# When sums and conversions are issued beside a chain of matrix products: one schedule change in a fused attention, mixture-of-experts and SoLU kernel

## Chip, cores and metric

The kernel runs on one core of one Trainium2 chip. The metric is device microseconds (us) of one execution, lower is better; several executions are timed and their median is given. TensorE is called PE in the profile, VectorE DVE, ScalarE ACT, GpSimd POOL, and SyncE, which only issues transfers here, SP.

## Reference, cut to what matters

Three layers follow one another: a local attention, a mixture of four experts in which every token goes through all experts, and a second layer with a softmax-gated normalisation. The change touches only how the weights of the last two layers are prepared.

```python
# mixture: N = 1536 tokens, D = 512, E = 4 experts, F = 1024
for e in range(E):
    h = np.maximum(x @ w1[e], 0.0)
    out += p[:, e:e + 1] * (h @ w2[e])
# second layer: its weights and g_ln arrive in float64
h = x @ w_in
...
return (ln @ w_out).astype(np.float32)      # ln = (solu - mu) / sqrt(var + 1e-06) * g_ln
```

## The kernel before

**Numbers in two parts.** Every product runs in three matmuls: each operand is split into a rounded high part and the rest (`split_of`, L275: the rounding is an ACT copy, L279, the rest a POOL subtraction, L287). A weight piece is 128 x 512; eight pieces make a half expert: four called R (first product, tiles `wR`) and four called V (second product, `wV`).

**A half expert.** `moe` (L598) walks over eight half experts, `he` = 0 to 7. For `he` of 1 and more the issue order is 23 groups of 12 matmuls, numbered 1 to 23 here. Groups 1 to 4 are the first product of the last 512 tokens (`g1`, L450); after each, ACT takes the rectified high part out of PSUM (L456) and VectorE the rest (L457). Groups 5 to 8 are the second product of the same tokens (`g2`, L469); it reads all four results, the fourth from its tenth and eleventh matmul on. VectorE scales what comes out of PSUM (L479) and POOL adds it to the running sum (L480). Groups 9 to 15 are the first product of the other 1024 tokens, done as seven products of half-size blocks instead of eight (`paired_groups`, L496, matmuls L530, evictions L517, L518, L535, L538). It needs sums and differences of weight blocks, the S pieces: `form_steps` (L312) loads two copies of weight pieces into `sc_b`, takes four sums on POOL (L328 to L331) and splits the two results (two ACT roundings, `ha` and `hb`, two POOL subtractions, `la` and `lb`). There are two such sets for each half expert. Groups 16 to 23 are the second product of those 1024 tokens, again L469, L479, L480.

**Conversions.** The second layer's weights arrive as 64-bit patterns. `conv_steps` (L341) brings 32 pieces to two-part form: load, four VectorE instructions (`one`, L189 to L192), three more (`two`, L196 to L198), for the last sixteen pieces a scaling by `gt` on ACT (L359), rounding on ACT (L360), the rest on VectorE (L363), store. Load and store are issued from ACT's queue.

**Order.** Each engine runs its instructions in the order in which the program issues them, so the order is written out by hand. After each group `tick` (L371) issues whatever side work is due: one step of each list in `st.work` (the S sets, and the splits of R and V pieces), loads of further pieces (`load_piece`, three raw buffers), loads of the second layer's weights (`load_second`) and, where the tick is not `quiet`, one step of each running conversion. Before the change the ticks of the paired groups are quiet except one, all others are not; a conversion starts every 3 or 4 ticks that are not quiet. Loads of weights, of S sets and of `pb` go through SP's queue. In the list of a half expert the first S set has its sums in tick 21 and its roundings in tick 22 and in tick 1 of the next half expert; the second set has its sums in tick 2 of the next half expert, its `ha` in tick 3 and its `hb` in tick 5.

Of the kernel before, what the change touches and what calls it, by code (L numbers as in the profile page):

```python
# [8 lines left out]
F32 = mybir.dt.float32  # L9
# [5 lines left out]
AF = mybir.ActivationFunctionType  # L15
# [35 lines left out]
def kernel(ctx, tc, ep, qk, vp, nn, pr, wall, w64, gl, out):  # L51
# [150 lines left out]
    def stream(arm):  # L202
# [9 lines left out]
        st.next_load = 0  # L212
        st.used = 0
        st.next_split = 0
        st.forms = []
        st.second = []
        st.free = {}
        st.hp = None
# [72 lines left out]
        def split_steps(hi_eng="act", lo_eng="pool", wait=0):  # L291

            if not ready(wait):
                return None
            n = st.next_split
            st.next_split += 1
            w = st.pieces[n] = place(n)
            steps = split_of(st.raws.pop(n), w, hi_eng, lo_eng)
            if n < 8:
                st.used += 1  # L300
                return steps

            def release():
                st.used += 1

            def both():
                for f in steps:
                    f()

            return [both, release]  # L310

        def form_steps(n):  # L312

            q = n % 8
            a, b = sc_b[q:q + 2]
            wa, wb = st.wS[:, q], st.wS[:, q + 1]
            st.pieces["S", n], st.pieces["S", n + 1] = wa, wb
            g, lo, hi = nc.gpsimd, slice(0, 256), slice(256, 512)

            def load():  # L320
                nc.sync.dma_start(out=a, in_=wall[n])
                nc.sync.dma_start(out=b, in_=wall[n + 1])

            def nothing():
                pass

            def sums():
                g.tensor_tensor(out=b[:, hi], in0=b[:, lo], in1=b[:, hi], op=ALU.add)  # L328
                g.tensor_tensor(out=b[:, lo], in0=a[:, lo], in1=b[:, lo], op=ALU.subtract)
                g.tensor_tensor(out=a[:, lo], in0=b[:, hi], in1=a[:, lo], op=ALU.subtract)  # L330
                g.tensor_tensor(out=a[:, hi], in0=a[:, hi], in1=a[:, lo], op=ALU.subtract)  # L331

            ha, la = split_of(a, wa, "act", "pool")
            hb, lb = split_of(b, wb, "act", "pool")
            return [load, nothing, nothing, sums, ha, la, hb, lb]

        def split_piece(hi_eng, lo_eng):
            for f in split_steps(hi_eng, lo_eng) or ():
# [2 lines left out]
        def conv_steps():  # L341

            c = st.next_conv
            if c >= 32 or st.cvp is None:
                return None
            st.next_conv += 1
            raw = st.cvp.tile([128, 256], I64, tag="r64", name=f"{arm}r64", bufs=2)
            one, two, ff, halves = from_f64(raw)

            def load():  # L350
                nc.scalar.dma_start(out=raw, in_=w64[c])

            def nothing():
                pass

            def high():
                if c >= 16:
                    j = (c - 16) // 2
                    nc.scalar.activation(ff, ff, AF.Copy, scale=gt[:, j:j + 1])  # L359
                nc.scalar.copy(halves[:, 0], ff)  # L360

            def low():
                nc.vector.tensor_tensor(out=halves[:, 1], in0=ff, in1=halves[:, 0].bitcast(F32), op=ALU.subtract)  # L363

            def store():
                nc.scalar.dma_start(out=w_dram[c // 2, :, :, 256 * (c % 2):256 * (c % 2) + 256], in_=halves.bitcast(F32))
                st.stored += 1

            return [load, nothing, one, two, high, low, store]

        def tick(split=True, quiet=False):  # L371

            st.now += 1
            for w in st.work:
                w.pop(0)()
            st.work = [w for w in st.work if w]
            if st.later and st.later[0][0] <= st.now:
                _, e, (c0, n) = st.later.pop(0)
                load_pb(e, c0, n)
            for at, n in st.forms:  # L380
                if at == st.now:
                    st.work.append(form_steps(n))
            if split:
                for _ in range(2):
                    w = split_steps(wait=2)
                    if w:
                        st.work.append(w)
            load_piece()
            load_piece()
            while st.second and st.stored >= 2 * st.second[0] + 2:  # L390
                load_second(st.second.pop(0))
            if not quiet:
                for w in st.conv:
                    w.pop(0)()
                st.conv = [w for w in st.conv if w]
                st.rest += 1
                if st.rest >= 4 - (st.next_conv % 2):
                    w = conv_steps()
                    if w:
                        st.conv.append(w)  # L400
                        st.rest = 0

        def drain():
            while st.work or st.second or st.conv:
                tick()

        st.tick = tick
# [88 lines left out]
        def paired_groups(he, h1, h2):  # L496
# [50 lines left out]
            for j in range(4):  # L547
                st.free["R", j] = he + 1
            if he < NHE - 1:
                st.forms += [(st.now + 2, 8 * he + 8), (st.now + 6, 8 * he + 10)]  # L550
            else:
                st.second += range(14)

# [32 lines left out]
                st.unformed.append(last)  # L586

        st.x_forms = x_forms
        st.paired_groups = paired_groups
        st.load_piece = load_piece  # L590
        st.split_piece = split_piece
# [6 lines left out]
    def moe(st, first_blocks):  # L598

        def run(he, blk, last, given=None):  # L600
            for gi, g in enumerate(st.gemm_groups(he, blk, last, given)):
                for cost in g:
                    yield 0, cost
                st.tick(st.wS is not None, quiet=he == 0)
            if he % 2 and he < NHE - 1:
                st.later.append((st.now + 2, he // 2 + 1, blk))

        for j, blk in enumerate(first_blocks):
            yield blk[0] + blk[1], 0.0
            if j == len(first_blocks) - 1:  # L610
                while st.unformed:
                    st.unformed.pop(0)()
            yield from run(0, blk, j == len(first_blocks) - 1)
        for he in range(1, NHE):
            yield from run(he, (2 * HALF, 512), False)
            h1, h2 = ([[None] * 4, [None] * 4] for _ in range(2))
            for i in st.paired_groups(he, h1, h2):
                yield 0, 0.0
                st.tick(quiet=i != 6)
            yield from run(he, (0, HALF), False, h1)  # L620
            yield from run(he, (HALF, HALF), True, h2)

    def rest_of_moe(st, arm, gen):
        with ExitStack() as es:
# [3 lines left out]
            st.ps3 = es.enter_context(tc.tile_pool(name=f"{arm}ps3a", bufs=1, space=PSUM))  # L628
            with tc.tile_pool(name=f"{arm}gps", bufs=6, space=PSUM) as psp:
                st.psp = psp  # L630
                st.forms += [(st.now + 1, 8), (st.now + 4, 10)]
                st.tick()
                for _ in gen:
                    pass
                st.drain()
# [619 lines left out]
```

## Time and profile before

| | |
|---|---|
| median of 3 runs | 793.01 us (792.77 to 793.44) |
| the profiled execution: its own time | 792.17 us |
| its span, first to last instruction | 790.4 us |
| PE busy | 754.5 us (95%) |
| DVE, ACT, POOL busy | 521.5, 286.4, 334.6 us |
| mean granted PE clock | 0.982 of full speed |

How to read it: the profile is one execution. A busy PE counts any time in which a matmul is in flight, so 95% says that its idle time is 36 us in all, not that it runs at its peak. The groups of L469 and L450 follow one another without a gap at 2.72 us each; half experts begin at 173.5, 236.3, 304.3, 372.7, 438.7, 508.6 and 580.8 us from the span's start, the second layer at 649.4 us.

### The profile page before, as it was taken

How to read it: one execution, taken by the hardware profiler on the slowest of the kernel's cores; microseconds unless marked ns; L12 is line 12 of the kernel's file. 1: busy time of each engine (PE TensorE's matmuls, PEld its weight loads, DVE VectorE, ACT ScalarE, POOL GpSimd, SP SyncE). 2: the span in 40 equal slices, each digit the busy share in tenths (PEclk: the TensorE clock that was granted, in tenths of full speed). 3: DMA queues.
4: the chain of work that ended last, by engine and by line, in shares of the span. 5: the costliest groups of instructions: out<-in, count | busy, mean ns of one | idle time of the engine just before them, and what ended most of it. 6: DMA issues, size and time to landing. Idle time of an engine off the chain costs nothing. (4 is left out here: it accounts for less than half of the span.)

```text
span 790.4 us, 10575 instructions
## 1 busy us (share of the span) xinstructions
PE 754.5 (95%) x3710; PEld 600.8 (76%) x3710; DVE 521.5 (66%) x1004; ACT 286.4 (36%) x641; POOL 334.6 (42%) x310
## 2 busy tenths in 40 slices
PE   8889999999998999899899899979998999999997
PEld 5667766688886888688688678858886787888886
DVE  6776788424587588758968765886696665565542
ACT  5676655332413232141332224132332423232442
POOL 1000089284079248607825840872498173000000
PEclk9999999999999999999999989979999999999999
DMA  8442421032144024314413221430231561122221
GB/s 248 140 128 79 122 80 54 1 97 64 40 133 134 27 82 132 93 27 134 133 39 106 96 80 41 148 105 27 95 107 40 177 261 40 51 73 64 74 74 45
DMA packets 54015, 73.01 MB, mean 92 GB/s; under 512 B 7104, under 2 KB 31936, under 8 KB 53952
## 3 DMA queue, kind: packets, MB, share of 16 engines
q1 hardware_dynamic: 40080, 55.03, 22.4%
q10 hardware_dynamic: 13872, 17.21, 6.9%
q8 instruction: 31, 0.51, 0.3%
q14 instruction: 32, 0.26, 0.1%
HBM read 56.46 MB, written 11.56 MB: 86 GB/s over the span
## 5 line engine op out<-in xcount | busy, mean ns | idle before, releaser
L469 PE MATMUL fg<-fhh,wV 128*128 128x512 f32 (+1 forms) x800 | 259.6, 396 | 9.2 <-ACT fhh L456 9.2
L480 POOL TENSOR_TENSOR scr<-scr,tmp 128x512 f32<-128x512 f32 x84 | 112.4, 1340 | 202.8 <-DVE tmp L479 202.7
L469 PEld LDWEIGHTS fg<-fhh,wV 128*128 128x128 f32 x800 | 154.8, 194 | 47.7 <-ACT fhh L456 12.3
L469 PE MATMUL fg<-fhl,wV 128*128 128x512 f32 (+1 forms) x400 | 158.5, 396 | 11.1 <-DVE fhl L457 11.1
L450 PE MATMUL fg<-xh,wR 128*128 128x512 f32 (+1 forms) x320 | 102.6, 387 | 1.4 <-DVE xl L894 1.4
L469 PEld LDWEIGHTS fg<-fhl,wV 128*128 128x128 f32 x400 | 77.4, 194 | 30.4 <-DVE fhl L457 16.2
L479 DVE TENSOR_TENSOR tmp<-fg,pb 128x512 f32<-128x512 f32 x84 | 57.0, 684 | 34.6 <-PE fg L469 32.0
L450 PEld LDWEIGHTS fg<-xh,wR 128*128 128x128 f32 x320 | 59.9, 188 | 17.1 <-issue 4.3
L838 ACT ACTIVATE p<-p,mn 128x256 f32<-128x256 f32 (+1 forms) x96 | 46.4, 484 | 41.3 <-DVE mn L832 38.8
L450 PE MATMUL fg<-xl,wR 128*128 128x512 f32 (+1 forms) x160 | 60.6, 379 | 0.0
L530 PE MATMUL fg<-xt,fwS 128*128 128x512 f32 x252 | 58.4, 390 | 0.9 <-ACT kr L535 0.9
L530 PEld LDWEIGHTS fg<-xt,fwS 128*128 128x128 f32 x252 | 47.2, 188 | 11.1 <-ACT kr L535 1.3
L530 PE MATMUL fg<-xh,wR 128*128 128x512 f32 x168 | 55.1, 394 | 0.0
L538 DVE TENSOR_TENSOR kr<-kr,fg 128x512 f32<-128x512 f32 x42 | 28.6, 682 | 34.7 <-ACT kr L535 27.5
L711 POOL TENSOR_SCALAR fva<-fva 128x1 f32<-128x1 f32 x12 | 3.7, 312 | 109.3 <-ACT scr L710 109.3
L457 DVE SCALAR_TENSOR_TENSOR fhl<-fg,fhh 128x512 fp32r<-128x512 f32 (+1 forms) x40 | 26.4, 660 | 35.4 <-ACT fhh L456 35.4
L518 DVE SCALAR_TENSOR_TENSOR fhl<-kr,fhh 128x512 fp32r<-128x512 f32 x42 | 29.1, 692 | 29.3 <-ACT fhh L517 29.3
L287 POOL TENSOR_TENSOR wR<-fraw,wR 128x512 fp32r<-128x512 f32 x28 | 38.6, 1389 | 16.8 <-ACT wR L279 16.8
L517 ACT ACTIVATE fhh<-kr 128x512 fp32r<-128x512 f32 x42 | 26.6, 632 | 51.9 <-DVE kr L538 51.9
L722 PE MATMUL fo<-xt,fth 128*128 128x512 f32 (+1 forms) x156 | 45.3, 375 | 0.0
L279 ACT CAST fwS<-kr 128x512 fp32r<-128x512 f32 x28 | 17.3, 617 | 69.2 <-POOL kr L331 66.5
L197 DVE SCALAR_TENSOR_TENSOR kr<-fr,kr 128x256 f32<-128x256 uint32 x32 | 41.5, 1295 | 1.1
(156 smaller groups left out, 1408.0 us busy)
## 6 DMA issues: line engine op xcount, KB each, us to landing
fraw<-in_wall_dram SPq DMA_DIRECT2D x61, 256.0 KB, 2.7
fr<-in_w_dram ACTq DMA_DIRECT2D x32, 256.0 KB, 2.7
w_dram<-fr ACTq DMA_DIRECT2D x32, 256.0 KB, 2.4
kr<-in_wall_dram SPq DMA_DIRECT2D x28, 256.0 KB, 2.8
v<-in_vp_dram SPq DMA_DIRECT2D x10, 512.0 KB, 3.4
xt<-w_dram SPq DMA_DIRECT2D x6, 512.0 KB, 9.2
kr<-in_qk_dram SPq DMA_DIRECT2D x22, 128.0 KB, 3.8
out_dram<-scr SPq DMA_DIRECT2D x11, 256.0 KB, 2.2
```

The costliest lines, as they stand in the source:

```text
L197: v.scalar_tensor_tensor(out=af, in0=low, scalar=2.0 ** -52, in1=af, op0=ALU.mult, op1=ALU.mult)
L287: e.tensor_tensor(out=w[:, 1], in0=t, in1=w[:, 0].bitcast(F32), op=ALU.subtract)
L450: nc.tensor.matmul(ps[:, :n], lhsT=w[:, a, k], rhs=b[:, k, cols], start=(k == 0 and i == 0), stop=(k == 3 and i == 2))
L469: nc.tensor.matmul(ps[:, :n], lhsT=w[:, a, k], rhs=b[k], start=(k == 0 and i == 0), stop=(k == 3 and i == 2))
L479: nc.vector.tensor_tensor(out=t, in0=ps[:, :n], in1=pb[:, cols], op=ALU.mult)
L480: nc.gpsimd.tensor_tensor(out=a, in0=a, in1=t, op=ALU.add)
L517: nc.scalar.activation(th, src, AF.Relu)
L518: nc.vector.scalar_tensor_tensor(out=tl, in0=src, scalar=0.0, in1=th.bitcast(F32), op0=ALU.max, op1=ALU.subtract)
L530: nc.tensor.matmul(ps, lhsT=w[:, a, j], rhs=x[b][j], start=(i in (1, 2, 5) and j == 0 and m == 0), stop=(j == 1 and m == 2), skip_group_ch ...
L538: nc.vector.tensor_tensor(out=t, in0=t, in1=banks[q, "b" if i == 2 else "c"], op=ALU.add)
L722: nc.tensor.matmul(ps, lhsT=a[:, fc % 4], rhs=wo[fc][:, b, c0:c0 + n], start=(fc == 0 and i == 0), stop=(fc == 7 and i == 2))
L838: nc.scalar.activation(p[:, a, :nw], p[:, a, :nw], AF.Exp, bias=mn[:, a:a + 1], scale=-1.0, accum_out=su[:, a:a + 1])
```

## The change

It does five things. (1) The S sets get fixed ticks, counted from the end of the paired groups: loads in ticks 16 and 17, sums in 19 and 20, the four roundings in 21 and 22, and the four subtractions in ticks 1 to 4 of the next half expert. (2) Conversions run on VectorE alone: the scaling by `gt` becomes a VectorE multiplication, the rounding a VectorE copy; the seven steps become six. (3) Their loads and stores move from ACT's queue to SP's. (4) A conversion starts every 3 ticks that are not quiet, and ticks 2 and 3 of each half expert become quiet as well. (5) The split of an R or V piece gives its raw buffer back one tick later.

```diff
+            return [both, nothing, release]
-        def form_steps(n):
+        def form_steps(n, at):
...
             ha, la = split_of(a, wa, "act", "pool")
             hb, lb = split_of(b, wb, "act", "pool")
-            return [load, nothing, nothing, sums, ha, la, hb, lb]
+            later = q // 2
+            for t, f in ((1 + later, load), (4 + later, sums), (6 + later, ha), (6 + later, hb),
+                         (9 + 2 * later, la), (10 + 2 * later, lb)):
+                st.due.setdefault(at + t, []).append(f)
...
             def load():
-                nc.scalar.dma_start(out=raw, in_=w64[c])
+                nc.sync.dma_start(out=raw, in_=w64[c])
...
-            def high():
+            def both():
+                two()
                 if c >= 16:
                     j = (c - 16) // 2
-                    nc.scalar.activation(ff, ff, AF.Copy, scale=gt[:, j:j + 1])
-                nc.scalar.copy(halves[:, 0], ff)
+                    nc.vector.tensor_scalar(ff, ff, gt[:, j:j + 1], None, op0=ALU.mult)
-            def low():
+            def parts():
+                nc.vector.tensor_copy(out=halves[:, 0], in_=ff)
                 nc.vector.tensor_tensor(out=halves[:, 1], in0=ff, in1=halves[:, 0].bitcast(F32), op=ALU.subtract)
             def store():
-                nc.scalar.dma_start(out=w_dram[c // 2, :, :, 256 * (c % 2):256 * (c % 2) + 256], in_=halves.bitcast(F32))
+                nc.sync.dma_start(out=w_dram[c // 2, :, :, 256 * (c % 2):256 * (c % 2) + 256], in_=halves.bitcast(F32))
-            return [load, nothing, one, two, high, low, store]
+            return [load, nothing, one, both, parts, store]
...
-                if st.rest >= 4 - (st.next_conv % 2):
+                if st.rest >= 3:
...
             if he < NHE - 1:
-                st.forms += [(st.now + 2, 8 * he + 8), (st.now + 6, 8 * he + 10)]
+                for q in (0, 2):
+                    form_steps(8 * he + 8 + q, st.now)
...
-                st.tick(st.wS is not None, quiet=he == 0)
+                st.tick(st.wS is not None, quiet=he == 0 or (given is None and gi in (1, 2)))
...
-                st.forms += [(st.now + 1, 8), (st.now + 4, 10)]
+                for q in (0, 2):
+                    st.form_steps(8 + q, st.now + 2)
```

In `tick` the lines that started S sets from `st.forms` give way to `for f in st.due.pop(st.now, ()): f()`, and `drain` also waits for `st.due`.

## Rows read from the trace of the kernel before

**Rows 1.** The page: the span, and busy time of PE and its loads.

```profile
span 790.4 us, 10575 instructions
...
PE 754.5 (95%) x3710; PEld 600.8 (76%) x3710; DVE 521.5 (66%) x1004; ACT 286.4 (36%) x641; POOL 334.6 (42%) x310
```

**Rows 2.** Windows, groups 5 to 8: stretch, length, engines' busy (instructions), PE clock, DMA.

```profile
184.40:195.28 10.88, 10.88 (x49) 9.01 (x48) 6.48 (x10) 0.60 (x1) 4.12 (x4) 1.00 0.22 73
247.13:263.30 16.17, 13.07 (x49) 10.13 (x48) 11.11 (x16) 2.24 (x4) 11.25 (x11) 0.89 0.27 81
315.17:331.70 16.53, 12.94 (x49) 10.02 (x48) 11.95 (x17) 2.03 (x4) 13.27 (x12) 0.90 0.31 89
383.57:397.68 14.11, 12.02 (x49) 8.77 (x48) 13.32 (x19) 3.15 (x6) 10.57 (x10) 1.00 0.33 93
449.53:467.65 18.12, 14.62 (x49) 10.45 (x48) 12.18 (x20) 3.44 (x8) 13.28 (x12) 0.81 0.26 77
519.52:539.86 20.34, 14.68 (x49) 10.55 (x48) 16.48 (x22) 4.40 (x9) 13.32 (x12) 0.75 0.26 79
591.71:607.22 15.51, 13.20 (x50) 10.00 (x48) 12.12 (x18) 3.68 (x7) 12.86 (x12) 0.89 0.10 34
```

**Rows 3.** Waits of PE: line, releaser, us in total, times, longest.

```profile
PE fg L469 <- DVE fhl L457: 11.1, 10, 3.7
PE fg L469 <- ACT fhh L456: 9.2, 4, 3.4
```

**Rows 4.** Timeline of ACT: start, us, instruction, idle before and its releaser.

```profile
250.93 0.62 ACT L279 CAST fwS<-kr 128x512 fp32r<-128x512 f32 x1 [5.65 <-POOL kr L331]
...
251.56 0.60 ACT L456 ACTIVATE fhh<-fg 128x512 fp32r<-128x512 f32 x1
```

**Rows 5.** Timelines of POOL and DVE while both are busy.

```profile
377.95 1.34 POOL L287 TENSOR_TENSOR wV<-fraw,wV 128x512 fp32r<-128x512 f32 x1
...
376.77 1.37 DVE L189 TENSOR_SCALAR kr<-fr 128x256 int32<-128x256 int32 x1
378.17 1.40 DVE L190 SCALAR_TENSOR_TENSOR kr<-fr,kr 128x256 int32<-128x256 int32 x1
...
521.12 0.83 DVE L190 SCALAR_TENSOR_TENSOR kr<-fr,kr 128x256 int32<-128x256 int32 x1
```

**Rows 6.** One line: durations in ns, smallest, median and largest.

```profile
L196 DVE TENSOR_SCALAR kr<-kr x32: 275/283/993, 193.7 to 642.4; 128x256 int32<-128x256 int32 x32
```

**Rows 7.** Windows in which DVE hardly waits; columns as in the second group.

```profile
353.97:372.69 18.72, 18.72 (x84) 15.49 (x83) 16.95 (x24) 2.67 (x5) 13.97 (x12) 1.00 0.45 142
375.56:385.28 9.72, 9.08 (x41) 7.18 (x39) 9.54 (x9) 2.84 (x5) 9.56 (x9) 1.00 0.48 135
```

**Rows 8.** Groups by line: busy us, mean ns, idle before and releasers.

```profile
L480 POOL TENSOR_TENSOR scr<-scr,tmp 128x512 f32<-128x512 f32 x84 | 112.4, 1340 | 202.8 <-DVE tmp L479 202.7
...
L287 POOL TENSOR_TENSOR wR<-fraw,wR 128x512 fp32r<-128x512 f32 x28 | 38.6, 1389 | 16.8 <-ACT wR L279 16.8
...
L331 POOL TENSOR_TENSOR kr<-kr 128x256 f32<-128x256 f32 x14 | 10.5, 750 | 1.1
...
L360 ACT CAST fr<-kr 128x256 fp32r<-128x256 f32 x32 | 13.0, 407 | 56.1 <-DVE kr L198 55.6
```

**Rows 9.** DMA issues: transfer, queue, count, KB each, median us to landing.

```profile
fr<-in_w_dram ACTq DMA_DIRECT2D x32, 256.0 KB, 2.7
w_dram<-fr ACTq DMA_DIRECT2D x32, 256.0 KB, 2.4
```

**Rows 10.** Timelines of PE and DVE where a paired stretch ends.

```profile
350.93 0.39 PE L469 MATMUL fg<-fhh,wV 128*128 128x512 f32 x1
...
353.37 0.69 DVE L518 SCALAR_TENSOR_TENSOR fhl<-kr,fhh 128x512 fp32r<-128x512 f32 x1 [0.70 <-ACT fhh L517]
353.97 0.68 DVE L479 TENSOR_TENSOR tmp<-fg,pb 128x512 f32<-128x512 f32 x1
```

**Rows 11.** Timeline of PE in the last half expert's paired groups.

```profile
613.73 2.56 PE L530 MATMUL fg<-xt,fwS 128*128 128x512 f32 x10 [0.91 <-ACT kr L535]
```

More of the change, by code (lines that the diff above doesn't have):

```diff
@@ L214, in stream @@
         st.next_split = 0
-        st.forms = []
+        st.due = {}
         st.second = []
@@ L308, in both, with nothing @@
                     f()
-            return [both, release]
-        def form_steps(n):
+            return [both, nothing, release]
+        def nothing():
+            pass
+        def form_steps(n, at):
             q = n % 8
@@ L322, in load @@
                 nc.sync.dma_start(out=b, in_=wall[n + 1])
-            def nothing():
-                pass
             def sums():
@@ L350, in load @@
             def load():
-                nc.scalar.dma_start(out=raw, in_=w64[c])
-            def nothing():
-                pass
-            def high():
+                nc.sync.dma_start(out=raw, in_=w64[c])
+            def both():
+                two()
                 if c >= 16:
                     j = (c - 16) // 2
-                    nc.scalar.activation(ff, ff, AF.Copy, scale=gt[:, j:j + 1])
-                nc.scalar.copy(halves[:, 0], ff)
-            def low():
+                    nc.vector.tensor_scalar(ff, ff, gt[:, j:j + 1], None, op0=ALU.mult)
+            def parts():
+                nc.vector.tensor_copy(out=halves[:, 0], in_=ff)
                 nc.vector.tensor_tensor(out=halves[:, 1], in0=ff, in1=halves[:, 0].bitcast(F32), op=ALU.subtract)
             def store():
-                nc.scalar.dma_start(out=w_dram[c // 2, :, :, 256 * (c % 2):256 * (c % 2) + 256], in_=halves.bitcast(F32))
+                nc.sync.dma_start(out=w_dram[c // 2, :, :, 256 * (c % 2):256 * (c % 2) + 256], in_=halves.bitcast(F32))
                 st.stored += 1
-            return [load, nothing, one, two, high, low, store]
+            return [load, nothing, one, both, parts, store]
         def tick(split=True, quiet=False):
@@ L379, in tick @@
                 load_pb(e, c0, n)
-            for at, n in st.forms:
-                if at == st.now:
-                    st.work.append(form_steps(n))
+            for f in st.due.pop(st.now, ()):
+                f()
             if split:
@@ L403, in drain @@
         def drain():
-            while st.work or st.second or st.conv:
+            while st.work or st.second or st.conv or st.due:
                 tick()
@@ L588, in stream @@
         st.x_forms = x_forms
+        st.form_steps = form_steps
         st.paired_groups = paired_groups
```

## The prediction, made before the changed kernel was run

> **What bounds the kernel now.** I read the page first: PE is busy for 754.5 of 790.4 us [rows 1], so nothing can gain unless PE idles less or runs at a higher clock. The windows then show where it does not. In groups 5 to 8 of the first half expert after the warm-up, 48 matmuls take 10.88 us, 0.227 us each; the same groups of the next six half experts take 14.11 to 20.34 us [rows 2]. Their sum is 100.78 us against 6 x 10.88 = 65.28, a loss of 35.5 us, and the matmuls before and after these stretches run without gaps. Inside them PE idles 20.25 us (length less PE busy, the same rows); the other 15.25 us are slow matmuls: the granted clock falls to between 0.75 and 0.90 in five of the six. So one microsecond of idle costs 35.5 / 20.25 = 1.75 us. This is the stage to argue about, and 35.5 us is nearly all that there is.
>
> The waits of PE name two releasers in these groups, VectorE with 11.1 us and ACT with 9.2 us [rows 3]. Groups 5 to 8 read what ACT (L456) and VectorE (L457) took out of PSUM in groups 1 to 4, and the reader is to see what stands in front of these two lines. On ACT it is a rounding of an S set: it sat 5.65 us until POOL's fourth sum, and the fourth L456 came right behind it at 251.56 [rows 4]. On VectorE it is conversion steps.
>
> **What a conversion step costs.** Its instructions have 256 elements. L196 takes 0.28 us at best and 0.99 at worst [rows 6], others 1.4. Rows 5 show why they are long: a VectorE instruction that begins while POOL works ends 0.2 to 0.3 us after that POOL instruction does. So beside a busy POOL one step goes through per POOL instruction: 1.4 us beside a 512-wide one, 0.83 beside the sums. The evictions, which have one operand in PSUM, take 0.68 and follow one another at about 0.61, as their records overlap (353.37 to 353.97) [rows 10].
>
> Two windows give the rate. With POOL busy three quarters of the time, 24 instructions took 16.95 us; less 8 evictions at 0.61 that is 12.07 us for 16 steps, 0.75, or 0.78 with the 0.03 us between two. With POOL busy throughout, 9.54 us less one eviction is 8.93 for 8 steps, 1.12, or 1.15 with the gap [rows 5, 7]. These are the two ends.
>
> **Edit by edit. The S sets.** They take the same instructions as before; only their places move. Before, the second set's sums stood in tick 2, behind POOL's backlog, and its rounding in front of the fourth L456. Now the sums stand in ticks 19 and 20. What POOL has to do before they end is five L480 at 1.34, three splits at 1.39, two sets of sums (3.0 us each, four times 0.75): 6.7 + 4.2 + 6.0 = 16.9 us, from 3.8 us after the paired groups end. That is 21 us, and some 2 more for waits on L479. The roundings of ticks 21 and 22 then run at 19 to 25 us, when ACT has nothing else but R and V roundings. The first L456 can start at 9 x 2.72 = 24.5 and the fourth at 32.6, so there are 8 us of cover [rows 8]. ACT's part of the idle time, 9.2 us, goes; and what is late next is VectorE.
>
> **ACT's conversion work.** ACT loses 32 x 0.407 = 13.0 us of roundings and the sixteen scalings; it is busy for only 36% of the span [rows 1, 8], so that is worth nothing by itself. What counts is that it no longer sits on VectorE's L198 in front of L456.
>
> **VectorE's.** It gains 32 copies and 16 multiplications. Nothing like them is in the trace; nearest is L196 with one input, 0.28 to 0.99 [rows 6], so 13 to 48 us in all, and I take the step rates above. Did they pass beside POOL at 0.28, the count below would end 3 x 0.7 = 2 us sooner, and 4 us with multiplications: rival (b). The Trainium skill, "SBUF — State Buffer", section "Who interferes with whom", speaks against that: a copy or `tensor_scalar` in a two-port mode, like an instruction with two SBUF inputs, takes turns with GpSimd on a shared port pair. The long durations of L196 agree. Before, 8 VectorE instructions came per 3.5 ticks; now 9 come per 3 (10 for the last sixteen pieces).
>
> Count what VectorE must finish before the fourth L457. By the new order ticks 16 to 23 hold `one`, `both`, `parts`, `one`, `both`, `parts`, `one`, `both` and tick 1 holds `parts`: 27 steps, or 30 with the multiplications, and ticks 2 and 3 are quiet. Beside them are 8 L479 and 4 L457. The first starts 3.1 us after the paired groups (353.37 + 0.69 - 350.93) [rows 10]. Some 9 steps fall in the first three ticks at 0.78, 8 beside the eight sums at 0.85, 10 beside POOL's subtractions and additions at 1.15: 7.0 + 6.8 + 11.5 = 25.3 us. With multiplications it is 10, 8 and 12: 28.4 us. The 12 evictions are 7.3. VectorE ends at 3.1 + 25.3 + 7.3 = 35.7, or 38.8 us. PE wants the fourth L457 at 12 x 2.72 + 10 x 0.227 = 34.9 us. It idles 0.8 us, or 3.9; at 1.75 that is 1.4 and 6.8 us.
>
> The multiplications start with the sixteenth piece. At five conversions per half expert they weigh on the stalls of half experts 5, 6 and 7 and not on those of 2, 3 and 4: 3 x 1.4 + 3 x 6.8 = 24.6 us. Against 35.5 the change saves 10.9 us.
>
> **Transfers.** 64 transfers move from ACT's queue to SP's. A conversion's load needs the buffer of the store one tick ahead of it, so SP stands for 2.4 us behind the store, which itself waits for `parts` [rows 9]. Queued behind it are weight loads. The latest is that of V pieces 3 and 4 in tick 1: it follows the load of tick 23, which waits for the store of tick 22 and so for the `parts` of tick 21, some 25 us after the paired groups. The store is done at 28, the load landed at 31; their rounding in tick 4 comes at 33 and the product needs the third V piece at 38.1. SP's wait is hidden by 5 to 7 us. The later return of raw buffers falls under the same cover. I cost both at nothing; if the cover went, each late microsecond would stop groups 7 and 8.
>
> **The tail.** In the last half expert PE idles 0.91 us on an L535 that was queued on ACT behind POOL's additions and the last S set [rows 11]. The set is done earlier now; I take 1 us, between nothing and the 1.6 that idle time costs at 1.75.
>
> **Sum.** The profiled execution took 792.17 us for its span of 790.4, 0.84 below the median. 792.17 - 10.9 - 1.0 = 780.3, and 781 us on the scale of the medians.
>
> **Rivals.** (a) *VectorE becomes the bound, and it is slower.* The steps saved on ACT land on the engine that already holds PE up. If every step after the first three ticks costs 1.15, VectorE ends at 3.1 + 7.0 + 18 x 1.15 + 7.3 = 38.1 us, or with multiplications 3.1 + 7.8 + 20 x 1.15 + 7.3 = 41.2. PE idles 3.2 and 6.3 us, 5.6 and 11.0 with the clock, 49.8 in six stretches: 14.3 us lost, 1 back, 806 us. For it speaks that POOL was busy for 9.56 of 9.72 us in such a stretch [rows 7], and that the sums now stand in front of the same evictions; against it, that the sums' steps cost 0.85. It decides from a mean step of about 0.985 instead of 0.94. The Trainium skill, "Perfetto Trace Analysis", section "Optimizing Scalar/DVE Operations", says the same as a rule: with a saturated DVE, work goes to Scalar, and this change does the opposite. VectorE at 66% is not saturated on the page [rows 1], but is in this stretch. Chance 0.2.
>
> (b) *The stalls vanish.* At 0.78 throughout VectorE ends at 31.5 or 33.8 us, before 34.9, and all of 35.5 + 1 goes: 756.5 us. For it speaks that ACT's share was half of the idle time and that ticks 2 and 3 are quiet; against it the second of rows 7. Between its stalls and mine all values can occur, 757 to 768. Chance 0.22.
>
> (c) *It does not do what it says:* the gain in the first three half experts is eaten by the last three, and the time stays within 0.2% (about what a measurement of this kernel can tell from no change), 791.4 to 794.6. That needs a mean step of about 0.98. Chance 0.08.
>
> (d) *SP holds the weights back.* If `parts` of tick 21 ended 6 us later than I count, V pieces 3 and 4 would come late in six half experts, at 2 us each some 12 x 1.75 = 21 us on top of the forecast, 802 us. Chance 0.04.
>
> **Numbers.** The forecast, part of the stalls left to VectorE, 768 to 791, has 0.46 and gives 781. Faster by over 0.2% is it and (b): 0.68. Within is (c): 0.08. Slower is (a) and (d): 0.24. The range runs from 762, which leaves out the better half of (b), to 802, which leaves out the worse half of (a): 0.8 inside.
>
> **What would show it.** ACT's roundings of S sets end before each first L456, and PE has no wait on L456 in groups 5 to 8. The waits of PE on L457 stay, larger after 440 us than before. VectorE's steps in ticks 19 to 23 take 0.8 to 1.4 us. The six windows take 12 to 13 us in the first three half experts and 17 to 18 in the last three. I am wrong if the six are alike (then the multiplications do not matter), if they take 10.88 (the rate is 0.78 or less), or if the idle time has a releaser other than VectorE.

## Result, and the profile after

The changed kernel takes 774.96 us (773.89 to 775.56, 4 runs) against 792.89 us (792.64 to 793.44, 4 runs) for the kernel before on the same chip: 0.9771 of it, 95% interval 0.9754 to 0.9788. It is faster by 2.3%; 781 was forecast, and the time lies in the range. The profiled execution took 773.89 us. Some lines of the changed kernel have numbers up to three higher than before, but those named here in groups 1 to 23 (L450 to L538) have kept theirs. The page, beside [rows 1]:

```profile
span 772.0 us, 10562 instructions
...
PE 746.5 (97%) x3710; PEld 597.9 (77%) x3710; DVE 565.2 (73%) x1052; ACT 264.9 (34%) x593; POOL 337.7 (44%) x310
```

VectorE works 43.7 us more than before, and yet the span is 18.4 us shorter. The windows of groups 5 to 8, with the columns of [rows 2]:

```profile
246.87:258.20 11.33, 11.18 (x49) 8.93 (x48) 11.12 (x15) 1.63 (x3) 8.94 (x8) 1.00 0.37 115
310.05:321.37 11.32, 11.16 (x49) 8.93 (x48) 11.11 (x15) 1.63 (x3) 8.94 (x8) 1.00 0.38 117
373.23:384.56 11.33, 11.18 (x49) 8.93 (x48) 11.12 (x15) 1.62 (x3) 8.95 (x8) 1.00 0.40 115
436.41:453.65 17.24, 13.95 (x50) 10.65 (x48) 16.22 (x24) 1.62 (x3) 11.50 (x9) 0.80 0.29 92
505.50:520.26 14.76, 11.50 (x49) 8.86 (x48) 14.46 (x21) 1.62 (x3) 10.24 (x9) 1.00 0.31 92
572.11:589.73 17.62, 14.32 (x49) 10.91 (x48) 17.18 (x23) 2.86 (x5) 13.58 (x11) 0.81 0.15 45
```

The six together take 83.60 us where they took 100.78, so 17.2 of the 18.3 us between the two profiled executions come from here; 1.2 more come from the last half expert's paired groups (20.43 us before, 19.21 after). The first three stretches lose 0.45 us each against 10.88, the last three 6.4, 3.9 and 6.7. PE's waits, to be read beside [rows 3]: no L456 any more.

```profile
PE fg L469 <- DVE fhl L457: 10.0, 7, 1.7
```

Where PE stops, in its timeline (start, us, instruction, idle before it and the releaser):

```profile
438.36 0.50 PE L469 MATMUL fg<-fhl,wV 128*128 128x512 f32 x1 [1.55 <-DVE fhl L457]
...
441.05 0.80 PE L469 MATMUL fg<-fhl,wV 128*128 128x512 f32 x1 [1.74 <-DVE fhl L457]
...
507.43 0.50 PE L469 MATMUL fg<-fhl,wV 128*128 128x512 f32 x1 [1.54 <-DVE fhl L457]
...
510.11 0.50 PE L469 MATMUL fg<-fhl,wV 128*128 128x512 f32 x1 [1.72 <-DVE fhl L457]
```

ACT's timeline answers to [rows 4]. The roundings of the S sets still wait for POOL (15.33 us for the first), but the second pair is through before the first L456, and the fourth L456 waits for PE's product alone:

```profile
423.07 1.14 ACT L279 CAST fwS<-kr 128x512 fp32r<-128x512 f32 x2 [15.33 <-POOL kr L331]
...
427.90 1.14 ACT L279 CAST fwS<-kr 128x512 fp32r<-128x512 f32 x2 [2.64 <-POOL kr L331]
...
429.47 0.59 ACT L456 ACTIVATE fhh<-fg 128x512 fp32r<-128x512 f32 x1
...
436.67 0.60 ACT L456 ACTIVATE fhh<-fg 128x512 fp32r<-128x512 f32 x1 [2.18 <-PE fg L450]
```

And VectorE's timeline ahead of the same matmuls:

```profile
435.02 1.40 DVE L198 TENSOR_TENSOR kr<-kr 128x256 f32<-128x256 f32 x1
436.45 1.25 DVE L360 TENSOR_SCALAR kr<-kr,gt 128x256 f32<-128x256 f32 x1
437.62 0.68 DVE L457 SCALAR_TENSOR_TENSOR fhl<-fg,fhh 128x512 fp32r<-128x512 f32 x1
438.22 0.76 DVE L363 CAST fr<-kr 128x256 fp32r<-128x256 f32 x1
439.02 1.37 DVE L364 TENSOR_TENSOR fr<-kr,fr 128x256 fp32r<-128x256 f32 x1
440.32 1.87 DVE L457 SCALAR_TENSOR_TENSOR fhl<-fg,fhh 128x512 fp32r<-128x512 f32 x3
```

The first L457 has the step `both` with its multiplication in front of it, the second the step `parts`; the third and fourth follow without a step between. So PE stops twice, for the first and the second result, 3.3 us in all.

### The profile page after: what moved, and what is told of

It reads as the page before. It is cut to its first block, busy times and chain, and to the rows that moved or that the text cites. A ratio compares the mean times of both kernels' runs of the same rounds, so it can differ in the third digit from the quotient of the medians.

```text
span 772.0 us, 10562 instructions
## 1 busy us (share of the span) xinstructions
PE 746.5 (97%) x3710; PEld 597.9 (77%) x3710; DVE 565.2 (73%) x1052; ACT 264.9 (34%) x593; POOL 337.7 (44%) x310
## 4 chain that ended last, share of the span: by engine, by line
PE 62%; DVE 21%; issue 9%; ACT 4%; POOL 3%; DMA 0%; DVEq 0%; POOLq 0%; ACTq 0%
PE fg L469 19%; PE fg L530 13%; PE fo L725 9%; PE fh L664 7%; PE fg L450 5%; DVE tmp L479 4%; PE sps L816 3%; PE x L885 3%; DVE kr L190 3%; DVE kr L197 2%; PE pt L863 2%; DVE kr L191 2%; POOL scr L480 2%; DVE fhl L518 1%; POOL xl L483 1%
## 5 line engine op out<-in xcount | busy, mean ns | idle before, releaser
L469 PE MATMUL fg<-fhh,wV 128*128 128x512 f32 (+1 forms) x800 | 255.1, 391 | 0.0
L469 PEld LDWEIGHTS fg<-fhh,wV 128*128 128x128 f32 x800 | 152.5, 191 | 35.2 <-issue 6.3
L469 PE MATMUL fg<-fhl,wV 128*128 128x512 f32 (+1 forms) x400 | 155.7, 389 | 10.3 <-DVE fhl L457 10.0
L450 PE MATMUL fg<-xh,wR 128*128 128x512 f32 (+1 forms) x320 | 102.7, 387 | 1.4 <-DVE xl L897 1.4
L469 PEld LDWEIGHTS fg<-fhl,wV 128*128 128x128 f32 x400 | 76.5, 191 | 28.4 <-DVE fhl L457 14.1
L450 PEld LDWEIGHTS fg<-xh,wR 128*128 128x128 f32 x320 | 59.9, 188 | 17.1 <-issue 4.3
L450 PE MATMUL fg<-xl,wR 128*128 128x512 f32 (+1 forms) x160 | 60.6, 379 | 0.0
L841 ACT ACTIVATE p<-p,mn 128x256 f32<-128x256 f32 (+1 forms) x96 | 46.3, 484 | 41.1 <-DVE mn L835 38.6
L530 PE MATMUL fg<-xt,fwS 128*128 128x512 f32 x252 | 58.3, 389 | 0.0
L535 ACT COPY kr<-fg 128x512 f32<-128x512 f32 x42 | 23.8, 581 | 97.3 <-PE fg L530 95.7
L530 PE MATMUL fg<-xh,wR 128*128 128x512 f32 x168 | 55.1, 394 | 0.0
L530 PEld LDWEIGHTS fg<-xt,fwS 128*128 128x128 f32 x252 | 47.3, 188 | 9.8
L287 POOL TENSOR_TENSOR wR<-fraw,wR 128x512 fp32r<-128x512 f32 x28 | 39.9, 1433 | 18.2 <-ACT wR L279 18.2
L517 ACT ACTIVATE fhh<-kr 128x512 fp32r<-128x512 f32 x42 | 26.6, 632 | 59.3 <-DVE kr L538 59.3
L190 DVE SCALAR_TENSOR_TENSOR kr<-fr,kr 128x256 int32<-128x256 int32 x32 | 43.3, 1353 | 1.1
L538 DVE TENSOR_TENSOR kr<-kr,fg 128x512 f32<-128x512 f32 x42 | 28.6, 681 | 20.3 <-ACT kr L535 18.8
```

What stands on the lines that cost most here:

```text
L190: v.scalar_tensor_tensor(out=f, in0=high, scalar=-2 ** 30, in1=a, op0=ALU.bitwise_and, op1=ALU.bitwise_or)
L287: e.tensor_tensor(out=w[:, 1], in0=t, in1=w[:, 0].bitcast(F32), op=ALU.subtract)
L450: nc.tensor.matmul(ps[:, :n], lhsT=w[:, a, k], rhs=b[:, k, cols], start=(k == 0 and i == 0), stop=(k == 3 and i == 2))
L469: nc.tensor.matmul(ps[:, :n], lhsT=w[:, a, k], rhs=b[k], start=(k == 0 and i == 0), stop=(k == 3 and i == 2))
L530: nc.tensor.matmul(ps, lhsT=w[:, a, j], rhs=x[b][j], start=(i in (1, 2, 5) and j == 0 and m == 0), stop=(j == 1 and m == 2), skip_group_ch ...
L538: nc.vector.tensor_tensor(out=t, in0=t, in1=banks[q, "b" if i == 2 else "c"], op=ALU.add)
```

## Experiments

Unless a diff says otherwise, each is the changed kernel with one thing altered. Times are medians; the ratio is to the kernel before on the same chip (792.47 us for the first four, 793.39 for the next four, 792.8 for the rest).

**Sums alone.** The kernel before with part (1) of the change: fixed ticks for the S sets, and nothing else.

```diff
-            return [load, nothing, nothing, sums, ha, la, hb, lb]
+            later = q // 2
+            for t, f in ((1 + later, load), (4 + later, sums), (6 + later, ha), (6 + later, hb),
+                         (9 + 2 * later, la), (10 + 2 * later, lb)):
+                st.due.setdefault(at + t, []).append(f)
```

> The kernel before with the S sets at their new ticks and nothing else changed: conversions keep their ACT steps, their cadence and ACT's queue, and ticks 2 and 3 are not quiet. My theory: the ACT half of the stalls was the wait on the second set's sums and goes, and what is left is VectorE's queue. About 26 conversion steps then stand before the fourth L457, 26 x 0.94 + 7.3 + 3.1 = 34.8 us plus 1 to 2 us in which VectorE waits for ACT's rounding, against 34.9 wanted: 1 to 2 us idle per stretch, six stretches at 12.5 to 15 us, 781 us, within 776 to 788, PE waiting on L457. Rival, that ACT was held up by the conversions (L359 and L360 behind L198) at least as much as by the sums: PE still waits on L456 in groups 5 to 8 by several us in total, and the time is 786 to 793.

797.42 us, ratio 1.0061 (1.0041 to 1.0081): slower than before by 0.6%, and 16 us above the 781 that I expected. No wait of PE names ACT any more, as expected, but VectorE's has taken its whole place and more (L458, L459 and L471 here are L456, L457 and L469):

```profile
PE fg L471 <- DVE fhl L459: 24.6, 10, 4.1
```

The reason stands in VectorE's timeline. Ticks 2 and 3 are not quiet here, so steps lie between one L459 and the next; in the first stretch a whole step of four instructions, 4.8 us beside a busy POOL, lies between the third and the fourth:

```profile
246.50 0.69 DVE L459 SCALAR_TENSOR_TENSOR fhl<-fg,fhh 128x512 fp32r<-128x512 f32 x1
247.11 0.77 DVE L189 TENSOR_SCALAR kr<-fr 128x256 int32<-128x256 int32 x1
247.91 1.39 DVE L190 SCALAR_TENSOR_TENSOR kr<-fr,kr 128x256 int32<-128x256 int32 x1
249.34 1.24 DVE L191 TENSOR_SCALAR kr<-fr 128x256 int32<-128x256 int32 x1
250.61 1.36 DVE L192 SCALAR_TENSOR_TENSOR kr<-kr 128x256 f32<-128x256 int32 x1
251.90 0.68 DVE L459 SCALAR_TENSOR_TENSOR fhl<-fg,fhh 128x512 fp32r<-128x512 f32 x1
```

The rival has a small part that PE's waits hide: in five of the six stretches an L458 stood on ACT behind a conversion step that had waited for VectorE's L198, and VectorE's L459 then waited 0.4 to 1.0 us for that L458.

**Everything but the sums.** The changed kernel with the S sets in their old ticks and the old return of raw buffers.

```diff
-            later = q // 2
...
+            return [load, nothing, nothing, sums, ha, la, hb, lb]
```

> The changed kernel with the S sets back at their old ticks and the raw buffers given back as early as before; conversions on VectorE alone, on SP's queue, every 3 ticks, ticks 2 and 3 quiet. My theory: the rounding of the second set stands again in front of the fourth L456 and waits for sums that end some 36 us after the paired groups, so the six stretches lose 4 to 7 us each through L456: 788 to 796 us, about as slow as the kernel before. Rival, that moving the conversions off ACT is the greater part of the gain: under 782 us.

796.0 us, ratio 1.0044 (1.0029 to 1.0059), at the upper edge of the theory's range. PE now waits for ACT (L454 and L455 are L456 and L457):

```profile
PE fg L467 <- ACT fhh L454: 19.8, 6, 3.3
PE fg L467 <- DVE fhl L455: 3.1, 6, 0.9
```

So each half of the change by itself costs 3.5 to 5 us, and both together save 18. Two waits stood in front of the same matmuls, and the later of the two decides. That says why neither half gains, not why each loses. In the first, the 149 steps in front of the fourth L459 take 1.00 us each in the mean, against 0.92 for as many in the kernel before; in the second, the second set's sums end 36.9 to 38.1 us after the paired groups, against 35.8 to 37.3, and the last paired block takes 22.0 us instead of 20.4. What makes them so was not tested.

**No scaling.** The sixteen multiplications are left out, so the second layer's weights miss the factor g_ln.

```diff
-                    nc.vector.tensor_scalar(ff, ff, gt[:, j:j + 1], None, op0=ALU.mult)
```

> The changed kernel without the sixteen multiplications by gt on VectorE; the scaling of the last sixteen pieces is left out of the computation. My theory: the last three stretches of groups 5 to 8 (17.2, 14.8 and 17.6 us) become like the first three (11.3), as 27 steps instead of 30 end before the fourth L457: 5.9 + 3.5 + 6.3 = 15.7 us less than the changed kernel, 759 us, within 757 to 762. Rival, that something else makes the later half experts slower (transfers, the clock): under 5 us less, 770 to 775.

763.04 us, ratio 0.9622 (0.9596 to 0.9649). All six stretches take 11.31 to 11.37 us: it is the multiplications that make the last three long (the first line below is the window of the fourth). The total is 1.0 us above the expected range, because a stall appears that the changed kernel does not have: the last half expert's paired groups take 24.73 us instead of 19.2 (L532 is L535).

```profile
436.63:447.96 11.33, 11.19 (x50) 8.94 (x49) 11.12 (x15) 1.62 (x3) 8.95 (x8) 1.00 0.39 117
...
PE fg L527 <- ACT kr L532: 3.6, 1, 3.6
```

**No quiet ticks 2 and 3.**

```diff
-                st.tick(st.wS is not None, quiet=he == 0 or (given is None and gi in (1, 2)))
+                st.tick(st.wS is not None, quiet=he == 0)
```

> The changed kernel with ticks 2 and 3 of a half expert not quiet. My theory: some 6 more steps (6 us) stand before the fourth L457, so PE idles 6 to 9 us in each of the six stretches instead of 0.1 and 3.3, at 1.7 us of time each: 830 us, within 805 to 850, all of it on L457. Rival, that VectorE would have had room for them because the conversions are spread over 17 ticks instead of 15: under 785 us.

806.13 us, ratio 1.0174 (1.0150 to 1.0197), at the lower edge of the theory's range and 31 us above the changed kernel. Before the fourth L457 stand 32 to 36 steps; it ends 41.0 to 43.2 us after the paired groups end, and five stretches take 19.6 to 20.9 us. In the sixth, where the conversions have run out, it takes 10.88.

```profile
PE fg L469 <- DVE fhl L457: 30.6, 13, 4.4
```

**Transfers on ACT's queue; early release.** Two kernels, each with one of the parts that I had costed at nothing undone.

```diff
-                nc.sync.dma_start(out=raw, in_=w64[c])
+                nc.scalar.dma_start(out=raw, in_=w64[c])
...
-            return [both, nothing, release]
+            return [both, release]
```

> The changed kernel with the 64 loads and stores of the conversions back on ACT's queue; nothing else is altered. Theory (the move of the transfers is worth nothing): within 3 us of the changed kernel's 775 us, so 772 to 778; the six stretches keep their lengths, three near 11.3 us and three of 14 to 18 us, and PE's waits there stay on L457. Rival 1: SP's queue holds weights back in the changed kernel; then this one is faster, below 771 us. Rival 2: ACT, standing behind a store that waits for VectorE's last step, hands L456 over late; then PE waits on L456 again and the time is above 780 us.

> The changed kernel with the raw buffer of an R or V piece given back as early as before the change. Theory (the later return lies under cover): 772 to 778 us, stretches as in the changed kernel. Rival: the earlier return lets loads be issued that then wait on SP for POOL's subtraction of the piece before, and hold back what stands behind them on SP, sets of sums and conversions alike: 780 to 790 us, with longer stretches. A gain below 771 us would say that the later return costs something.

774.15 us (ratio 0.9764, 0.9742 to 0.9786) and 774.06 us (0.9758, 0.9732 to 0.9784): neither differs from the changed kernel, and in both the fourth L457 ends 35.0 and 38.4 us after the paired groups, as in it.

**Three ticks moved into the paired groups.**

```diff
-                st.tick(st.wS is not None, quiet=he == 0 or (given is None and gi in (1, 2)))
+                st.tick(st.wS is not None, quiet=he == 0 or (given is None and gi < 3) or (last and given is not None and gi > 1))
-                st.tick(quiet=i != 6)
+                st.tick(quiet=i not in (1, 2, 6, 5))
```

> The changed kernel with as many ticks that are not quiet, but three of them (tick 1 and the last two of a half expert) moved into the paired groups, after their first, second and fourth product. Theory (what is left of the loss is the number of VectorE steps that stand in front of the fourth L457): 18 to 20 steps instead of 27 or 30, the fourth L457 ends near 29 us after the paired groups end, PE has no wait on L457 in the six stretches, each takes 11.3 us, and the time is 757 to 763 us, no longer than without the multiplications. Rival: VectorE's evictions of the paired groups come late behind the steps put there; the stretches are short all the same, but the blocks of the paired groups grow by 2 us and more in each half expert, and the time is 770 us or above.

772.57 us, ratio 0.9738 (0.9718 to 0.9758). The first half of the theory held: 18 and 20 steps, all six stretches 10.88 us. (The fourth L457 ends at 34.2 us and not near 29, because PE has the fourth product ready only at 12 x 2.72 = 32.6.) The total did not hold; the rival's mechanism took it back. The steps behind the first two products stand on VectorE in front of the paired evictions, the paired blocks of half experts 2 to 6 take 20.7 to 22.3 us instead of 19.2, and the last takes 26.6:

```profile
PE fg L530 <- ACT kr L535: 13.0, 8, 4.5
```

**The scaling back on ACT.**

```diff
-                    nc.vector.tensor_scalar(ff, ff, gt[:, j:j + 1], None, op0=ALU.mult)
+                    nc.scalar.activation(ff, ff, AF.Copy, scale=gt[:, j:j + 1])
```

> The changed kernel with the sixteen scalings back on ACT, in the same step; VectorE keeps the roundings. Theory (VectorE's sixteen multiplications cost the three long stretches, and ACT has cover, because its fourth L456 starts as soon as PE has the product): all six stretches near 11.3 us, 760 to 768 us, near the 763 of the kernel without the scaling. Rival: the scaling waits on ACT for VectorE's L198 in front of L456, so PE waits on L456 and the three late stretches stay above 14 us: 773 us or more.

769.19 us, ratio 0.9689 (0.9666 to 0.9712): 5.8 us less than the changed kernel, between the theory's upper bound and the rival's lower. The three late stretches take 12.6 to 12.7 us instead of 14.8 to 17.6. The rival's mechanism is there, but small: ACT's scaling waits for VectorE's L198, and the first three L456 follow it, 31 us after the paired groups instead of from 25.7 on. The fourth still comes on PE's heel:

```profile
434.38 0.51 ACT L360 ACTIVATE kr<-kr,gt 128x256 f32<-128x256 f32 x1 [5.52 <-DVE kr L198]
434.80 1.55 ACT L456 ACTIVATE fhh<-fg 128x512 fp32r<-128x512 f32 x3
436.71 0.60 ACT L456 ACTIVATE fhh<-fg 128x512 fp32r<-128x512 f32 x1 [0.36 <-PE fg L450]
```

A second loss lies behind these stretches: the paired blocks of half experts 5 and 6 take 20.7 us instead of 19.2, and the last takes 24.4.

```profile
PE fg L530 <- ACT kr L535: 5.5, 3, 3.2
```

**Two ticks moved behind the later paired products.**

```diff
+                st.tick(st.wS is not None, quiet=he == 0 or (given is None and gi < 3) or (last and given is not None and gi > 2))
+                st.tick(quiet=i not in (6, 5, 4))
```

> The changed kernel with ticks 1 and 23 of a half expert made quiet too, and in their place the ticks after the fourth and the sixth product of the paired groups not quiet, where POOL has little to do and VectorE waits; as many ticks for conversions as in the changed kernel. Theory: 21 to 23 steps in front of the fourth L457, which ends at or before 34.5 us; the six stretches take 10.9 to 11.4 us as with the steps moved behind the first two products, but the paired blocks of half experts 2 to 6 stay at 19.2 us, because the new steps stand behind the evictions that the next product needs. The last half expert's paired block keeps a stall of 5 to 7 us: 760 to 765 us. Rival: any step in the paired groups holds its evictions back, blocks of 20.5 to 22 us: 769 us or more.

766.28 us, ratio 0.9672 (0.9654 to 0.9689). The six stretches and the paired blocks of half experts 2 to 6 are as expected: 10.90 to 11.43 us, and 19.21. What is left in the last three stretches has a new releaser, POOL's subtraction (L287) of the third V piece:

```profile
PE fg L469 <- POOL wV L287: 0.7, 3, 0.3
```

The total is 1.3 us above the range, since the last paired block takes 26.91 us (a wait of 4.8 us on L535) and the second layer's first group 13.3 instead of 12.1.

**That block's queue.** In the last half expert ACT rounds each result of groups 5 to 8 (L482) after POOL's sum, and L535 of the first paired product stands behind the fourth of these. Here L482 and L483 of groups 5 to 8 are issued six ticks later.

```diff
+                        def parts(a=a, dt=dt):
+                            nc.scalar.copy(xh[:, dt, cols], a)
...
+                            st.due.setdefault(st.now + 6, []).append(parts)
```

> The kernel before this one in the list, and in the last half expert the two-part form of the result of groups 5 to 8 (ACT's L482 and POOL's L483) issued six ticks later, so that ACT's L535 no longer queues behind L482. Theory (that stall is this queue and nothing else): the last half expert's paired block falls from some 25 us to 19 to 20 us, and the time to 755 to 760 us. Rival: POOL's four subtractions of 1.3 us only move the wait behind the paired groups, to the last product or the start of the second layer: no more than 1.5 us shorter than the kernel before it.

762.97 us, ratio 0.9627 (0.9610 to 0.9645): 3.3 us less than the kernel before it in this list, and 3 us above my range. L541 and L536 here are L535 and L530; the block falls to 23.41 us, not to 20. The deferred POOL subtractions (now L484) fall on the steps that the last kernel had put behind the paired products, where VectorE's steps had been cheap; beside POOL they cost up to 1.4 us, and the eviction L544 (L538 before) comes late:

```profile
585.79 1.40 DVE L198 TENSOR_TENSOR kr<-kr 128x256 f32<-128x256 f32 x1
587.23 1.26 DVE L360 TENSOR_SCALAR kr<-kr,gt 128x256 f32<-128x256 f32 x1
...
589.20 0.68 DVE L544 TENSOR_TENSOR kr<-kr,fg 128x512 f32<-128x512 f32 x1
```

**ACT's whole share back on ACT**, scaling and rounding, as a step of its own; sums, quiet ticks, queue and spacing as changed.

```diff
+            def high():
+                if c >= 16:
+                    j = (c - 16) // 2
+                    nc.scalar.activation(ff, ff, AF.Copy, scale=gt[:, j:j + 1])
+                nc.scalar.copy(halves[:, 0], ff)
...
+            return [load, nothing, one, both, high, parts, store]
```

> The changed kernel with ACT's whole share of a conversion back on ACT, the scaling and the rounding, as a step of their own (seven steps again); sums, quiet ticks, queue and spacing as changed. Theory (once the sums stand early and two ticks are quiet, ACT has the time, and VectorE is the late engine): 24 steps in front of the fourth L457, stretches of 10.9 to 12.7 us, 760 to 769 us. Rival (taking the roundings from ACT is part of the gain): ACT's rounding waits for VectorE's L198 in front of the last L456s, PE waits on L456 again, stretches of 14 us and more: 773 us or above.

763.96 us, ratio 0.9637 (0.9620 to 0.9654): 11 us faster than the changed kernel. There are 24 steps before the fourth L457, and each of the six stretches takes 10.88 us. In the order of seven steps tick 1 holds none of VectorE's, so the steps are fewer and also none stands behind the first product; the run does not separate the two. Nearly all that is left is the last paired block (windows: a stretch in half expert 5, and that block):

```profile
435.65:446.53 10.88, 10.88 (x50) 9.01 (x48) 10.71 (x14) 2.31 (x5) 8.65 (x7) 1.00 0.38 122
571.91:599.21 27.30, 21.98 (x86) 17.49 (x84) 14.56 (x22) 10.29 (x20) 8.58 (x7) 0.87 0.21 79
```

**Both.** ACT's share on ACT, and L482 and L483 of the last half expert's groups 5 to 8 nine ticks later, behind all conversion steps of its paired groups.

> The changed kernel with ACT's share of the conversions back on ACT, and in the last half expert the two-part form of groups 5 to 8 (one ACT copy and one POOL subtraction for each) issued nine ticks later, after the fifth to seventh products of the paired groups and the first group behind them. Theory (what that first edit leaves is one wait of 5.3 us behind this queue, with the slow matmuls after it): the last paired block falls from 27.3 us to 19.2 to 20 us, the six stretches stay at 10.88, and the time to 755 to 759 us. Rival: the deferred work is late for VectorE's and ACT's evictions of the last products or for the second layer, and gives most of it back: 761 us or above.

757.18 us (757.05 to 758.27), ratio 0.9558 (0.9539 to 0.9577), as expected and the best version: 35.6 us below the kernel before. The 8.2 us that the last paired block gains come out as 6.8 of the time: at the start of the second layer PE waits 2.7 us for VectorE, 1.3 in the kernel without the deferral. Its windows of the same two places:

```profile
435.64:446.52 10.88, 10.88 (x50) 9.02 (x48) 10.71 (x14) 2.31 (x5) 8.61 (x7) 1.00 0.38 122
571.91:591.06 19.15, 19.15 (x86) 15.65 (x84) 13.73 (x22) 8.95 (x17) 5.96 (x5) 1.00 0.31 109
```

## Why the prediction was right, and where it was off

**The bound and the S sets: right.** The loss sat where [rows 2] had it. The sums end 23.3 and 24.1 us after the paired groups (forecast: about 23), the roundings run before the first L456, and PE has no wait on L456. With the sums put back, 19.8 us of such waits return.

**VectorE next: right, almost to the number.** 27 and 30 steps stand before the fourth L457; their mean with the gap is 0.94 and 0.96 us (0.94 and 0.95 forecast). It ends at 35.0 and 38.4 us (35.7 and 38.8). What I had wrong is which result is late: PE stops at the first and the second L457, with the steps of ticks 23 and 1 in front of them, not at the fourth.

**The size of the loss: the mis-sized term is PE's idle time.** The stretches were put at 12.3 and 17.7 us and measured 11.33, and 17.24, 14.76 and 17.62, together 6.3 us less, which is about the distance from 781 to 775. Idle time was put at 0.8 us in each of the first three and 3.9 in each of the last three, 14.1 in all; it measured 0.15 and 3.3, 10.3 in all, because VectorE ends 0.7 and 0.4 us earlier than counted. At the forecast's own 1.75 these 3.8 us are 6.6. The factor itself came out in the sum (18.3 us lost for 10.3 us of idle time, 1.78), but that is luck: in the last three stretches 3.3 us of idle time cost 6.4, 3.9 and 6.7 us, and in one of them the granted clock did not fall.

**Multiplications weigh on the last three only: right**, shown by leaving them out.

**Conversions on VectorE: a loss that was never priced by itself.** The prediction says that moving ACT's work is worth nothing by itself and that what counts is that it leaves the queue in front of L456, and it counts VectorE's added steps only within one sum. The runs show that part of the edit to be a loss: with ACT's share on ACT and the rest kept, ACT's rounding does hold the second and third L456 back, but the fourth not, and the time falls by 11 us. So the right total hides one part of the change with the wrong sign, and the gain is that of the early sums together with the two quiet ticks (the spacing of 3 ticks was not tried by itself, nor the sums and quiet ticks without it). The Trainium skill, "Perfetto Trace Analysis", section "Optimizing Scalar/DVE Operations", says that work may go from a saturated DVE to Scalar; in these stretches the runs agree, 769.2 us with the scaling on ACT and 764.0 with all of it, against 775.0, though VectorE is busy for 73% of the span on the page.

**Quiet ticks: too little said.** I used them only in counting steps. They are worth 31 us here, and the sums alone, without them, make the kernel slower, which my expectation for that run missed too: there I took ACT's half of the idle time as saved and put the end of VectorE's queue at 34.8 us, while the fourth L459 ended 38.4 to 41.1 us after the paired groups.

**Transfers at nothing: right by the two runs that undid them, but with less cover than counted.** The 5 to 7 us of cover were counted up to ACT's rounding of V pieces 3 and 4. Behind it comes POOL's subtraction (L287), which the third matmul of group 7 reads: in the short stretches of the changed kernel the third piece's rounding ends 34.0 us after the paired groups, its subtraction 36.9, and that matmul starts at 39.0. So a transfer could have come some 3.7 us later (39.0 less 34.0, less 1.3 for the subtraction), and POOL 2.1. With two ticks moved behind the later paired products POOL itself was late, and PE waited for it.

**The tail.** 1.2 us came in the paired block, 1 was forecast. But it came by luck, because PE's stall just ahead covered a longer wait. With the transfers back on ACT's queue, or with the early release, the last stretch is 1.4 and 1.6 us shorter and that block 1.3 and 1.5 us longer. And wherever the last stretch loses under 2 us, with that queue left as it was, L535 behind the fourth L482 costs 2.2 to 5.3 us of waiting and 4 to 8 us of time. So rival (b) had the wrong price: its condition is all but met without the multiplications, and met with ACT's share on ACT, but these take 763 and 764 us; its 756.5 was reached (757.2) only once that queue was mended as well.

## What to carry to other kernels

When a matmul has two late operands, removing one wait can gain nothing, as here: price each edit by what is late next, since parts can lose alone and win together. Count the side work that is issued between the product and its eviction, step by step, since a step in the last places before a wanted eviction has no cover, while the same step elsewhere can be free (behind the fourth and sixth paired product it was, in half experts 2 to 6; behind the first two it was not). A gain in one stage can be eaten by a queue further on that the old stall had covered, so look at the first wait after each removed one.

## What the hardware showed that was not expected

**Equal waits, unequal clocks.** The stretches at 436.41, 505.50 and 572.11 us stop PE in the same two places for 3.3 us in all, after the same gapless groups. The granted clock there is 0.80, 1.00 and 0.81, and the cost differs by a factor of 1.7. In the two kernels that undid the transfers and the release, the same two waits in the last stretch (3.27 us) went with 0.89 and cost 5.2 to 5.4 us. What decides it was not found. In the best version, whose stretches have no stall, the mean granted clock is 1.000 over the whole span, against 0.982 before.

**Where a short instruction's time goes.** The trace of the changed kernel has 304 instructions of conversion steps on VectorE. The 107 that begin while POOL is idle take 0.28 to 0.36 us with one input and 0.42 to 0.43 with two. The other 197 begin while a POOL instruction runs, and every one of them ends behind that instruction: by 0.15 to 0.21 us with one input, by 0.28 to 0.29 with two. (The prediction's "0.2 to 0.3 us" joins the two.) So the new copy has a median of 0.286 us and the multiplication of 1.248, smallest 0.353, by where POOL happens to be. The groups by line, for the three kinds of step that end a conversion:

```profile
L364 DVE TENSOR_TENSOR fr<-kr,fr 128x256 fp32r<-128x256 f32 x32 | 35.0, 1093 | 1.1
L360 DVE TENSOR_SCALAR kr<-kr,gt 128x256 f32<-128x256 f32 x16 | 15.3, 956 | 0.6
L363 DVE CAST fr<-kr 128x256 fp32r<-128x256 f32 x32 | 13.5, 421 | 0.0
```

Before, the subtraction took 0.794 us in the mean (it is L363 there); with the copy ahead of it, 1.093. Copy and subtraction together are 0.72 us dearer than the subtraction alone, not the 0.29 us of a copy beside an idle POOL; the rest of the order differs between the two kernels too, so the copy's own part in this is not shown. The Trainium skill, "SBUF — State Buffer", section "Who interferes with whom", says that copies and `tensor_scalar`, where they run in a two-port mode, and instructions with two inputs in SBUF can contend with GpSimd for a shared port pair; the multiplication, 0.353 us at best and up to 1.40, agrees.
